# Linear attention and its MLP on one core: k and q of units six to eleven transposed by DMA instead of by TensorE, with a new order

## The chip, the cores and the metric

The kernel runs on one NeuronCore of a Trainium2 chip. TensorE (PE) multiplies matrices into PSUM, VectorE (DVE), ScalarE (ACT) and GpSimd (POOL) work element by element, and SyncE (SP) has no arithmetic of its own: its queue issues transfers, which sixteen DMA engines carry out. Each engine runs its own instructions strictly in the order in which the program gives them and waits at semaphores for the others. The metric is the device time of one execution in microseconds, as a median over runs.

## What is computed

For each of 4 x 8 heads a state of 48 x 48 is carried over 768 steps: it decays by a gate and takes in an outer product, and a query reads it. The 4 x 768 results, 384 numbers each, go through two matrices with a leaky relu between them.

```python
f = 1.0 / (1.0 + np.exp(-f_logit))
for t in range(S):                       # S = 768, D = 48
    state = f[:, :, t, :, None] * state + np.einsum('bhd,bhe->bhde', k[:, :, t], v[:, :, t])
    y[:, :, t] = np.einsum('bhd,bhde->bhe', q[:, :, t], state)
x = y.transpose(0, 2, 1, 3).reshape(B * S, H * D)     # 3072 x 384
h = x @ w_in                                          # 384 x 2048
out = np.maximum(0.01 * h, h) @ w_out                 # 2048 x 384
```

## The kernel before, in words

The sequence is cut into six chunks of 128 steps and the batch into two halves of two batch elements. A chunk of a half is a **unit**; there are twelve, numbered 0 to 11, and `pairs[j]` gives chunk and half of unit `j`. Within a chunk the recurrence becomes matrix products. A unit goes through these steps, each a short function whose name in the order stands in front of it:

- `Lf Lk Lq Lv` (`load`, L99): eight loads per unit, one for each of f, k, q, v and each batch element `a`, all in SyncE's queue. The tiles are ring buffers of six units.
- `gate` (ScalarE): logarithm of the gate. `cs` (TensorE, L141 and L144): its running sum over the chunk, by a product with a triangle of ones. `dec` (ScalarE): the exponentials of it, for k, for q, and for the end of the chunk.
- `k`, `q` (`scale_k` L160, `scale_q` L166): k and q are multiplied by these and rounded to bf16, into tiles `kh` and `qh` of 128 steps x 2 x 8 heads x 64 columns, of which 48 are used and the rest is zero. For units six to eleven GpSimd does both, one instruction for each unit and operand. `v` (`cast_v`, GpSimd) rounds v.
- `tk`, `tq` (`turn`, L187): the scores need k and q with the head's dimension on the partitions. TensorE transposes four blocks of 128 x 128 (two heads each) per batch element into PSUM; `ck`, `cq` (`turn_out`, L190) are VectorE's copies into the tiles `kT` and `qT`.
- `sc` (`score`, L206): products of `kT` and `qT`, for both batch elements of units from four on (`sc_6_2` is unit six, both). `mk` (VectorE, L211): the causal mask. `mx` (`mix`, L239): scores times v, and `qT` times the state from before the chunk. `xt` (VectorE): the result into `xT`.
- `pt` (L250), `sf` (VectorE), `sb` (GpSimd, L260 and L263): the state's update for the next chunk.
- `uu`/`pu` and, from unit four on, `up`/`pr`: the first matrix (L290, L277) and the leaky relu (ScalarE); `dn` (`down`, L300): the second matrix; `ob` (VectorE, L305) and `st` (L313): copy and store.

The weights come in seven pieces through GpSimd's queue (`W`, pieces 0 to 2 of the first matrix, 3 to 6 of the second), from the time when `v` of unit one has landed. `H` (`hold`) is a tiny transfer in SyncE's queue that reads the last bytes of a piece: all that stands behind it in the queue, which is the loads of units two and later, waits until that piece has landed.

Nothing here is scheduled by a tool at build time. `order` is one long text of words, each a call: `tk_6_0` calls `turn(6, 0, "k")`. The order of the words of one engine is that engine's order; between engines the words' order says nothing, the semaphores do. A function `turn_dma` with the words `xk` and `xq` is there and isn't called: it issues one transfer in SyncE's queue that transposes all of a unit's `kh` (or `qh`), 128 x 1024 bf16, straight into `kT` (or `qT`).

Of the kernel before, what the change touches and what calls it, by code (L numbers as in the profile page):

```python
# [15 lines left out]
def kernel(  # L16
# [342 lines left out]
    uu_1_1_3 q_2_0 st_0_0 dn_1_0_1 ob_0_1 sb_1_0 pu_1_1_3 Lf_3_0 k_2_0 tq_2_0 gate_2_1 dn_1_1_0 cq_2_0 sb_0_1 st_0_1
    tk_2_0 pt_2_0 pu_1_1_2 dn_1_1_1 ck_2_0 Lk_3_0 sf_2_0 sb_1_1 sc_2_0 cs_2_1 mk_2_0_1 Lq_3_0 dn_1_1_2 dec_2_1 v_2_1  # L360
    mk_2_0_0 dn_1_0_2 Lv_3_0 mx_2_0 k_2_1 Lf_3_1 gate_3_0 dn_1_0_3 xt_2_0 tk_2_1 q_2_1 Lk_3_1 uu_2_0_0 ck_2_1 tq_2_1
    Lq_3_1 pu_2_0_0 uu_2_0_1 cq_2_1 ob_1_0 cs_3_0 sc_2_1 Lv_3_1 dec_3_0 pt_2_1 mk_2_1_1 dn_1_1_3 st_1_0 mk_2_1_0
    dn_2_0_0 pu_2_0_1 q_3_0 k_3_0 gate_3_1 uu_2_0_2 Lf_4_0 v_3_0 sf_2_1 tq_3_0 tk_3_0 pu_2_0_2 Lk_4_0 dn_2_0_1 ck_3_0
    cq_3_0 cs_3_1 Lq_4_0 mx_2_1 dec_3_1 sc_3_0 xt_2_1 dn_2_0_2 Lv_4_0 k_3_1 q_3_1 uu_2_1_0 Lf_4_1 mk_3_0_0 uu_2_0_3
    v_3_1 pu_2_1_0 ob_1_1 Lk_4_1 pt_3_0 tq_3_1 pu_2_0_3 mk_3_0_1 tk_3_1 uu_2_1_1 st_1_1 ck_3_1 mx_3_0 sf_3_0 pu_2_1_1
    uu_2_1_2 Lq_4_1 cq_3_1 gate_4_0 xt_3_0 dn_2_1_0 Lv_4_1 pu_2_1_2 sc_3_1 cs_4_0 Lf_5_0 mk_3_1_1 uu_3_0_0 dec_4_0
    mk_3_1_0 dn_2_1_1 Lk_5_0 gate_4_1 mx_3_1 k_4_0 q_4_0 Lq_5_0 dn_2_1_2 xt_3_1 v_4_0 pu_3_0_0 cs_4_1 Lv_5_0 uu_3_1_0
    dec_4_1 sb_2_0 dn_2_0_3 Lf_5_1 pu_3_1_0 tk_4_0 q_4_1 ob_2_0 uu_3_1_1 Lk_5_1 ck_4_0 pt_3_1 tq_4_0 pu_3_1_1 sf_3_1
    dn_3_1_0 st_2_0 gate_5_0 uu_3_1_2 cq_4_0 k_4_1 Lq_5_1 pt_4_0 tq_4_1 pu_3_1_2 sf_4_0 cs_5_0 tk_4_1 Lv_5_1 dec_5_0
    uu_3_1_3 ck_4_1 cq_4_1 uu_2_1_3 Lf_6_0 pu_3_1_3 q_5_0 sc_4_2 pu_2_1_3 Lk_6_0 uu_3_0_1 sb_2_1 mk_4_1_1 gate_5_1  # L370
    dn_2_1_3 Lq_6_0 k_5_0 v_4_1 uu_3_0_2 pu_3_0_1 mk_4_0_0 Lv_6_0 dn_3_1_1 mk_4_0_1 v_5_0 pu_3_0_2 cs_5_1 mk_4_1_0
    Lf_6_1 tk_5_0 dec_5_1 uu_3_0_3 ob_2_1 Lk_6_1 mx_4_2 pu_3_0_3 k_5_1 q_5_1 st_2_1 tq_5_0 xt_4_0 dn_3_1_2 v_5_1
    ck_5_0 dn_3_0_0 Lq_6_1 xt_4_1 sb_3_0 tk_5_1 cq_5_0 tq_5_1 Lv_6_1 pt_4_1 ck_5_1 dn_3_0_1 sb_4_0 cq_5_1 Lf_7_0
    up_4_0 sf_4_1 dn_3_0_2 sb_3_1 Lk_7_0 pr_4_0 sc_5_2 Lq_7_0 up_4_1 mk_5_1_0 dn_3_0_3 mk_5_0_0 pr_4_1 Lv_7_0 up_4_2
    mk_5_0_1 gate_6_0 v_6_0 Lf_7_1 dn_3_1_3 mk_5_1_1 pt_5_0 up_4_3 Lk_7_1 pr_4_2 mx_5_2 pr_4_3 Lq_7_1 up_4_4 xt_5_0
    Lv_7_1 cs_6_0 sf_5_0 pr_4_4 up_4_5 ob_3_1 Lf_8_0 sb_5_0 dec_6_0 cs_6_1 up_4_6 xt_5_1 st_3_1 ob_3_0 pt_5_1 pr_4_5
    dn_4_0_0 pr_4_6 up_4_7 st_3_0 dec_6_1 dn_4_0_1 Lk_8_0 up_5_0 pr_4_7 q_6_0 Lq_8_0 dn_4_0_2 gate_7_0 Lv_8_0 up_5_1
# [2 lines left out]
    sf_6_0 pt_6_1 up_5_4 gate_8_0 Lf_9_0 k_7_0 sf_6_1 dn_4_1_0 Lk_9_0 sc_6_2 pr_5_4 up_5_5 q_7_0 Lq_9_0 mk_6_0_0  # L380
    dn_4_1_1 mk_6_0_1 pr_5_5 Lv_9_0 up_5_6 mk_6_1_1 v_7_0 tk_7_0 Lf_9_1 mk_6_1_0 pr_5_6 tq_7_0 dn_5_0_2 ck_7_0 sb_5_1
    Lk_9_1 pt_7_0 tk_7_1 sf_7_0 up_5_7 Lq_9_1 dn_4_1_2 v_8_0 cq_7_0 pr_5_7 ck_7_1 pt_7_1 tq_7_1 Lv_9_1 sf_7_1 cs_8_0
    dn_5_0_3 dec_8_0 cq_7_1 Lf_10_0 mx_6_2 ob_5_0 gate_9_0 st_5_0 dn_5_1_0 xt_6_0 sb_6_0 cs_8_1 xt_6_1 Lk_10_0
    dn_5_1_1 dec_8_1 sb_6_1 up_6_0 Lq_10_0 dn_5_1_2 pr_6_0 Lv_10_0 q_8_0 up_6_1 sc_7_2 Lf_10_1 pr_6_1 up_6_2 mk_7_0_0
    k_8_0 Lk_10_1 dn_5_1_3 mk_7_0_1 pr_6_2 up_6_3 Lq_10_1 mk_7_1_0 tq_8_0 mk_7_1_1 pr_6_3 up_6_4 Lv_10_1 cq_8_0 pt_8_0
    tk_8_0 pr_6_4 ob_5_1 up_6_5 Lf_11_0 sf_8_0 mx_7_2 pr_6_5 st_5_1 ck_8_0 gate_10_0 up_6_6 xt_7_0 Lk_11_0 dn_4_1_3
    xt_7_1 up_6_7 Lq_11_0 pr_6_6 tk_8_1 pr_6_7 tq_8_1 Lv_11_0 ck_8_1 cs_9_0 pt_8_1 ob_4_1 up_7_0 dec_9_0 Lf_11_1
# [2 lines left out]
    pr_7_5 dn_6_0_2 mk_8_1_0 up_7_6 sb_7_0 mk_8_0_0 dn_6_0_3 mk_8_0_1 pr_7_6 k_10_0 tq_9_0 mk_8_1_1 gate_11_0 dn_7_0_2  # L390
    cq_9_0 tq_9_1 mx_8_2 ob_6_0 v_9_0 cq_9_1 st_6_0 dn_6_1_0 xt_8_0 tq_10_0 xt_8_1 sb_7_1 tk_9_0 up_7_7 cq_10_0 ck_9_0
    tq_10_1 sb_8_0 pr_7_7 tk_9_1 cq_10_1 cs_11_0 pt_9_0 up_8_0 dec_11_0 ck_9_1 sf_9_0 dn_7_0_3 sc_9_2 ob_7_0 up_8_1
    mk_9_0_0 st_7_0 dn_7_1_0 mk_9_0_1 dn_6_1_1 mk_9_1_1 dn_7_1_1 mk_9_1_0 cs_11_1 dn_6_1_2 dec_11_1 dn_7_1_2 pr_8_1
# [46 lines left out]
```

## Time and profile before

| | us |
|---|---|
| median of 3 runs (lowest, highest) | 189.87 (189.79, 190.28) |
| the profiled execution | 189.33 |
| its span, first to last instruction | 187.5 |
| TensorE busy / weight loads | 173.9 / 137.9 |
| VectorE, ScalarE, GpSimd busy | 98.3, 99.1, 76.0 |

The page cuts the span into forty slices and shows each engine's busy share in tenths:

```profile
PE   0575899999999999999999999999999999999994
DMA  6999999499997998998998999971110100111122
```

and lists the costliest groups of instructions, with busy time, mean duration, and the idle time ahead of them and who ended it:

```profile
L187 PE MATMUL tp<-ident,kh 128*128 128x128 bf16 x96 | 10.2, 234 | 0.3 <-DVE kh L160 0.2
L187 PE MATMUL tp<-ident,qh 128*128 128x128 bf16 x96 | 10.2, 234 | 2.7 <-DVE qh L166 2.7
L190 DVE COPY kT<-tp 128x512 bf16<-128x512 bf16 x24 | 10.0, 419 | 8.0 <-PE tp L187 7.7
L190 DVE COPY qT<-tp 128x512 bf16<-128x512 bf16 x24 | 10.1, 419 | 7.3 <-PE tp L187 7.0
L160 POOL TENSOR_TENSOR kh<-k_raw,em_t 128x768 bf16<-128x768 f32 x6 | 9.9, 1647 | 7.7 <-issue 7.6
```

A group's busy time is the sum of its instructions' durations; matmuls overlap each other, so for TensorE it is more than the time that they hold the engine. The time of a transfer in the DMA list runs from its issue to its landing.

### The profile page before, as it was taken

The page shows a single profiled execution, that of the slowest core. Times are in us where ns is not written, and L with a number is a line of the kernel's source. Part 1 is how long each engine was busy: PE and PEld are TensorE (multiplying, and loading weights), DVE is VectorE, ACT ScalarE, POOL GpSimd, SP SyncE. Part 2 cuts the span into 40 slices and gives each one's busy share as a digit, 9 for nine tenths or more (in the row PEclk, how much of TensorE's full clock was granted, in tenths as well). Part 3 has the DMA queues.
Part 4 walks back from the last instruction along what each step waited for, and adds up shares of the span by engine and source line. Part 5 has one row for each costly group of instructions (what it writes and reads, how often), then busy time and mean ns, then how long its engine had stood idle before and what let it go on. Part 6 is the DMA issues. An engine that isn't in the chain of part 4 may idle for free.

```text
span 187.5 us, 5631 instructions
## 1 busy us (share of the span) xinstructions
PE 173.9 (93%) x2360; PEld 137.9 (74%) x2360; DVE 98.3 (52%) x212; ACT 99.1 (53%) x201; POOL 76.0 (41%) x138
## 2 busy tenths in 40 slices
PE   0575899999999999999999999999999999999994
...
DMA  6999999499997998998998999971110100111122
GB/s 122 208 207 187 207 213 194 94 188 249 178 237 168 195 223 157 207 209 170 251 233 168 211 192 201 238 147 42 47 45 0 42 5 3 42 42 45 42 84 84
DMA packets 106113, 27.10 MB, mean 145 GB/s; under 512 B 100456, under 2 KB 105192, under 8 KB 106088
## 3 DMA queue, kind: packets, MB, share of 16 engines
...
## 4 chain that ended last, share of the span: by engine, by line
PE 87%; DMA 6%; SPq 3%; issue 2%; POOL 1%; DVE 0%; POOLq 0%
PE po L300 32%; PE pm L277 23%; PE pm L290 13%; PE py L239 5%; PE tp L187 5%; DMA w_in_b<-in_moe_w_in_dram 4%; PE pw L206 3%; SPq L99 3%; DMA v_raw<-in_v_dram 2%; PE cs L141 2%; PE pt L250 2%; PE po L322 1%; PE cs L144 1%; POOL v_b L173 0%; POOL v L174 0%
## 5 line engine op out<-in xcount | busy, mean ns | idle before, releaser
L300 PE MATMUL po<-w_out_b,gT 128*128 128x384 bf16 x368 | 71.6, 326 | 0.0
L283 ACT ACTIVATE gT<-pm 128x512 bf16<-128x512 f32 x64 | 37.6, 598 | 36.0 <-PE pm L277 35.2
L277 PE MATMUL pm<-xT,w_in_b 128*128 128x256 bf16 x384 | 51.4, 273 | 0.0
L300 PEld LDWEIGHTS <-gT 128*128 128x128 bf16 x368 | 34.1, 98 | 16.0 <-issue 0.2
L277 PEld LDWEIGHTS <-w_in_b 128*128 128x128 bf16 x384 | 40.7, 114 | 4.7
L211 DVE TENSOR_TENSOR wm<-pw,ut 128x512 bf16<-128x512 f32 x48 | 30.6, 683 | 19.6 <-PE pw L206 19.4
L305 DVE COPY osb<-po 128x384 f32<-128x384 f32 x23 | 12.6, 551 | 34.4 <-PE po L300 34.3
L295 ACT ACTIVATE gT<-pm 128x512 bf16<-128x512 f32 x32 | 19.1, 595 | 16.5 <-PE pm L290 15.9
L290 PE MATMUL pm<-xT,w_in_b 128*128 128x128 bf16 x384 | 26.8, 225 | 0.5 <-DMA w_in_b<-in_moe_w_in_dram 0.5
L166 POOL TENSOR_TENSOR qh<-q_raw,a_t 128x384 bf16<-128x384 f32 (+1 forms) x12 | 15.7, 1310 | 27.0 <-ACT a_end L155 23.5
L290 PEld LDWEIGHTS <-w_in_b 128*128 128x128 bf16 x384 | 24.3, 116 | 2.3 <-DMA w_in_b<-in_moe_w_in_dram 0.7
L173 POOL CAST v_b<-v_raw 128x384 bf16<-128x384 f32 (+1 forms) x18 | 12.4, 690 | 25.7 <-DMA v_raw<-in_v_dram 25.4
L151 ACT ACTIVATE em_t<-cs 128x384 bf16<-128x384 f32 x24 | 11.7, 490 | 13.1 <-PE cs L144 8.2
L245 DVE CAST xT<-py 128x384 bf16<-128x384 f32 x24 | 12.7, 552 | 7.3 <-PE py L239 6.9
L135 ACT ACTIVATE e_t<-f_raw 128x384 f32<-128x384 f32 (+1 forms) x18 | 11.4, 631 | 9.2 <-DMA f_raw<-in_f_logit_dram 9.2
L263 POOL CAST sb<-sf 64x192 bf16<-64x192 f32 x40 | 14.2, 355 | 4.1 <-PE py L239 1.7
L141 PE MATMUL cs<-lf,ut 128*128 128x384 bf16 x24 | 8.5, 353 | 6.7 <-ACT lf L136 6.5
L190 DVE COPY kT<-tp 128x512 bf16<-128x512 bf16 x24 | 10.0, 419 | 8.0 <-PE tp L187 7.7
L190 DVE COPY qT<-tp 128x512 bf16<-128x512 bf16 x24 | 10.1, 419 | 7.3 <-PE tp L187 7.0
L260 POOL TENSOR_TENSOR sf<-sf,a_end 128x192 f32<-128x192 f32 x20 | 10.4, 518 | 8.0 <-DVE sf L256 7.5
L160 POOL TENSOR_TENSOR kh<-k_raw,em_t 128x768 bf16<-128x768 f32 x6 | 9.9, 1647 | 7.7 <-issue 7.6
L187 PE MATMUL tp<-ident,qh 128*128 128x128 bf16 x96 | 10.2, 234 | 2.7 <-DVE qh L166 2.7
...
## 6 DMA issues: line engine op xcount, KB each, us to landing
f_raw<-in_f_logit_dram SPq DMA_DIRECT2D x24, 192.0 KB, 4.0
k_raw<-in_k_dram SPq DMA_DIRECT2D x24, 192.0 KB, 3.8
q_raw<-in_q_dram SPq DMA_DIRECT2D x24, 192.0 KB, 3.9
v_raw<-in_v_dram SPq DMA_DIRECT2D x24, 192.0 KB, 4.0
out_dram<-osb SPq DMA_DIRECT2D x17, 192.0 KB, 3.2
w_out_b<-in_moe_w_out_dram POOLq DMA_DIRECT2D x4, 384.0 KB, 13.3
...
```

The costliest lines, as they stand in the source:

```text
L166: eng.tensor_mul(qhs[j % NR][:, a, :, 0:D], raw(j, "q")[:, a], st[j]["a"][:, a].rearrange("t a (h d) -> t a h d", d=D))
L187: nc.tensor.transpose(tp[:, p, :], scaled(j, x)[:, a, 2 * p:2 * p + 2, :], ident)
L190: nc.vector.tensor_copy(out=turned(j, x)[:, P2 * a:P2 * a + P2, :], in_=st[j].pop(("tp" + x, a)))
L211: nc.vector.tensor_mul(wm, st[j].pop(("pw", a, i)), ut[:, None, :].to_broadcast([128, P2, 128]))
L245: nc.vector.tensor_copy(out=xT[:, :, a, :], in_=st[j].pop(("py", a))[:, 0:NK, :])
L263: nc.gpsimd.tensor_copy(out=sb[rows, a, :, i * D:i * D + D], in_=sf[rows, a])
L277: nc.tensor.matmul(pm[:, i, :], w_in(kk, ff), st[j]["xT"][:, kk].rearrange("t a s -> t (a s)"), start=(kk == 0), stop=(kk == NK - 1))
L283: nc.scalar.activation(gT[:, 2 * g:2 * g + 2, :], st[j].pop(("pm", g)), AF.Prelu, alpha=0.01)
L290: nc.tensor.matmul(pm[:, i, :], w_in(kk, ff), st[j]["xT"][:, kk, a, :], start=(kk == 0), stop=(kk == NK - 1))
L295: nc.scalar.activation(gT[:, 4 * g:4 * g + 4, 128 * a:128 * a + 128], st[j].pop(("pu", a, g)), AF.Prelu, alpha=0.01)
L300: nc.tensor.matmul(po, st[j]["g"][:, ff, 128 * a:128 * a + 128], w_out_b[:, ff, :], start=(ff == 0), stop=(ff == NF - 1))
L305: nc.vector.tensor_copy(out=osb, in_=st[j].pop(("po", a)))
```

## The change

Units six to eleven use `xk` and `xq` in place of `tk`, `tq`, `ck` and `cq`: twelve DMA transposes in SyncE's queue. `kT` and `qT` have three buffers each and not two. The order of all words is another one, on every engine; in it `H_4` stands in place of `H_5`, and stores of units seven to nine that were cut in two (`st_7_1_2`) are mostly whole. `weights` and `hold` count the pieces of the first matrix by the list's length, which is three as before. The diff, with the order cut to some of its lines:

```diff
@@ -106,12 +106,12 @@
         if (x, j, a) not in seen:
             seen.add((x, j, a))
             nc.gpsimd.tensor_copy(out=gate_w[:, 0:1], in_=raw(j, "fkqv"[x])[0:1, a, H - 1, D - 1:D])
-        if piece < 3:
+        if piece < len(w_in_cols):
             lo, hi = w_in_cols[piece]
             nc.gpsimd.dma_start(out=w_in_b[piece], in_=moe_w_in[:, lo:hi].rearrange("(k p) n -> p k n", p=128))
         else:
             n = NF // 4
-            part = piece - 3
+            part = piece - len(w_in_cols)
             nc.gpsimd.dma_start(
                 out=w_out_b[:, part * n:(part + 1) * n, :],
                 in_=moe_w_out[part * n * 128:(part + 1) * n * 128, :].rearrange("(p a) n -> p a n", a=n))
@@ -120,10 +120,10 @@
 
     def hold(piece):
 
-        if piece < 3:
+        if piece < len(w_in_cols):
             src = w_in_b[piece][0:1, NK - 1, 0:4]
         else:
-            src = w_out_b[0:1, (piece - 2) * (NF // 4) - 1, 0:4]
+            src = w_out_b[0:1, (piece - len(w_in_cols) + 1) * (NF // 4) - 1, 0:4]
         nc.sync.dma_start(out=gate_s[:, 0:4], in_=src)
 
     def half(j, i):
@@ -176,7 +176,7 @@
                               .rearrange("t p (j e) -> t p j e", j=2))
 
     def turned(j, x):
-        return once(j, x + "T", lambda: work.tile([128, 2 * P2, 128], BF16, name=x + "T", tag=x + "T", bufs=2))
+        return once(j, x + "T", lambda: work.tile([128, 2 * P2, 128], BF16, name=x + "T", tag=x + "T", bufs=3))
 
     def scaled(j, x):
         return (khs if x == "k" else qhs)[j % NR]
@@ -346,63 +346,60 @@
 
 
     order = """
...
-    Lk_1_1 k_0_1 tq_0_1 Lq_1_1 mk_0_0_0 tk_0_1 mk_0_0_1 cs_1_0 Lv_1_1 cq_0_1 pt_0_1 dec_1_0 W_0_3_1_0 ck_0_1 mx_0_0
-    W_1_3_1_0 sc_0_1 xt_0_0 gate_1_1 sf_0_1 sb_0_0 q_1_0 cs_1_1 W_2_3_1_0 k_1_0 dec_1_1 tq_1_0 mk_0_1_0 W_3_3_1_0
...
-    uu_1_0_2 uu_1_1_1 pu_1_0_2 H_5 Lf_2_0 dn_0_0_1 pu_1_1_1 Lk_2_0 dn_0_1_1 Lq_2_0 dn_0_0_2 Lv_2_0 uu_1_0_3 Lf_2_1
...
-    k_6_0 dn_4_0_3 Lf_8_1 pr_5_0 tq_6_0 cs_7_0 pr_5_1 cq_6_0 tq_6_1 Lk_8_1 up_5_2 sf_5_1 sb_4_1 dec_7_0 dn_5_0_0
-    ob_4_0 Lq_8_1 up_5_3 pr_5_2 cq_6_1 st_4_0 tk_6_0 pr_5_3 cs_7_1 ck_6_0 tk_6_1 pt_6_0 dec_7_1 dn_5_0_1 Lv_8_1 ck_6_1
...
-    sf_8_1 cs_9_1 up_7_1 pr_7_0 cq_8_1 st_4_1 dn_6_0_0 pr_7_1 up_7_2 Lk_11_1 dec_9_1 dn_6_0_1 Lq_11_1 pr_7_2 cs_10_0
-    q_9_0 up_7_3 dec_10_0 Lv_11_1 cs_10_1 dn_7_0_0 pr_7_3 up_7_4 k_9_0 dec_10_1 dn_7_0_1 pr_7_4 up_7_5 q_10_0 sc_8_2
...
-    pr_9_2 dn_9_0_0 mk_10_1_0 pr_8_5 up_9_3 tk_11_1 pr_9_3 pt_9_1 up_9_4 ck_11_1 sf_9_1 dn_9_0_1 pr_9_4 sb_9_1 up_9_5
-    sc_11_2 pr_9_5 up_9_6 mk_11_0_0 dn_9_0_2 mk_11_1_1 pr_9_6 up_8_6 mk_11_0_1 up_9_7 mk_11_1_0 mx_10_2 pr_9_7 pr_8_6
...
+    mk_0_0_0 gate_1_0 Lk_1_1 q_0_1 mx_0_0 Lq_1_1 k_0_1 cs_1_0 xt_0_0 tq_0_1 Lv_1_1 dec_1_0 tk_0_1 cq_0_1 W_0_3_1_0
+    pt_0_1 ck_0_1 k_1_0 sc_0_1 sb_0_0 gate_1_1 q_1_0 tk_1_0 sf_0_1 W_1_3_1_0 mk_0_1_0 cs_1_1 W_2_3_1_0 dec_1_1
...
+    uu_1_0_1 pu_1_0_0 uu_1_1_0 pu_1_0_1 uu_1_1_1 pu_1_1_0 pu_1_1_1 dn_0_1_0 uu_0_0_2 dn_0_0_0 pu_0_0_2 uu_0_0_3 H_4
...
+    Lf_7_1 up_4_3 pr_4_2 k_6_0 sc_5_2 Lk_7_1 pr_4_3 up_4_4 mk_5_0_0 Lq_7_1 dn_4_0_1 q_6_0 mk_5_1_0 pr_4_4 xk_6 pt_6_0
+    mk_5_0_1 up_4_5 mk_5_1_1 pt_6_1 pr_4_5 up_4_6 xq_6 sf_6_0 mx_5_2 gate_7_0 sf_6_1 Lv_7_1 up_4_7 xt_5_0 sb_5_0
+    dn_4_0_2 Lf_8_0 xt_5_1 pr_4_6 cs_7_0 pr_4_7 up_5_0 dec_7_0 Lk_8_0 cs_7_1 dn_4_0_3 pr_5_0 up_5_1 Lq_8_0 ob_4_0
+    dec_7_1 dn_4_1_0 st_4_0 up_5_2 pr_5_1 q_7_0 sc_6_2 Lv_8_0 pr_5_2 dn_4_1_1 mk_6_0_0 Lf_8_1 up_5_3 sb_5_1 mk_6_1_1
...
+    mk_7_0_1 Lq_9_1 q_8_0 pr_5_7 up_6_5 mk_7_1_1 xk_8 dn_5_0_3 pr_6_5 mx_7_2 ob_5_0 xq_8 dn_6_0_2 gate_9_0 xt_7_0
+    sb_7_0 up_6_6 st_5_0 xt_7_1 pt_8_0 sb_7_1 up_7_0 sf_8_0 Lv_9_1 pr_6_6 pt_8_1 cs_9_0 pr_7_0 sf_8_1 up_7_1 dec_9_0
...
+    st_6_1 up_8_4 mk_9_0_0 dn_8_0_1 Lf_11_1 mk_9_1_0 sb_8_1 pr_8_4 up_8_5 xk_10 mk_9_1_1 pt_9_1 mk_9_0_1 dn_7_0_0
+    pr_8_5 Lk_11_1 sf_9_1 up_8_6 Lq_11_1 mx_9_2 pr_8_6 dn_8_0_2 xt_9_0 sb_9_0 Lv_11_1 up_8_7 xt_9_1 dn_7_0_1 q_10_0
+    pr_8_7 up_9_0 gate_11_0 dn_7_0_2 v_10_0 xq_10 dn_8_0_3 pr_9_0 dn_7_0_3 ob_8_0 sb_9_1 cs_11_0 up_9_1 st_8_0 ob_7_0
+    dec_11_0 dn_7_1_0 st_7_0 v_11_0 pr_9_1 cs_11_1 up_9_2 dec_11_1 dn_9_0_0 pr_9_2 q_11_0 sc_10_2 up_9_3 mk_10_1_0
+    dn_7_1_1 mk_10_1_1 pr_9_3 k_11_0 xq_11 up_9_4 mk_10_0_0 dn_7_1_2 mk_10_0_1 pr_9_4 up_9_5 xk_11 mx_10_2 pr_9_5
+    dn_9_0_1 xt_10_0 up_9_6 xt_10_1 dn_7_1_3 pr_9_6 up_10_0 ob_7_1 sc_11_2 st_7_1 pr_10_0 up_10_1 mk_11_0_1 up_9_7
...
```

More of the change, by code (lines that the diff above doesn't have):

```diff
@@ L354 @@
-    cq_1_1 tk_1_1 uu_0_0_0 mk_1_0_0 ck_1_1 uu_0_1_0 pu_0_0_0 mk_1_0_1 sc_1_1 pu_0_1_0 mk_1_1_0 uu_0_0_1 mx_1_0
-    pu_0_0_1 pt_1_0 xt_1_0 uu_0_1_1 mk_1_1_1 uu_1_0_0 pu_0_1_1 mx_1_1 pu_1_0_0 uu_1_0_1 xt_1_1 pt_1_1 sf_1_0 pu_1_0_1
-    uu_0_0_2 sf_1_1 uu_0_1_2 pu_0_0_2 pu_0_1_2 uu_0_1_3 uu_0_0_3 pu_0_1_3 dn_0_0_0 pu_0_0_3 uu_1_1_0 dn_0_1_0 pu_1_1_0
-    uu_1_0_2 uu_1_1_1 pu_1_0_2 H_5 Lf_2_0 dn_0_0_1 pu_1_1_1 Lk_2_0 dn_0_1_1 Lq_2_0 dn_0_0_2 Lv_2_0 uu_1_0_3 Lf_2_1
-    uu_1_1_2 gate_2_0 Lk_2_1 dn_0_1_2 dn_0_0_3 pu_1_0_3 Lq_2_1 cs_2_0 ob_0_0 dn_0_1_3 dec_2_0 Lv_2_1 dn_1_0_0 v_2_0
@@ L359 @@
[L359 to L377, printed above, removed]
-    k_6_0 dn_4_0_3 Lf_8_1 pr_5_0 tq_6_0 cs_7_0 pr_5_1 cq_6_0 tq_6_1 Lk_8_1 up_5_2 sf_5_1 sb_4_1 dec_7_0 dn_5_0_0
@@ L379 @@
-    ob_4_0 Lq_8_1 up_5_3 pr_5_2 cq_6_1 st_4_0 tk_6_0 pr_5_3 cs_7_1 ck_6_0 tk_6_1 pt_6_0 dec_7_1 dn_5_0_1 Lv_8_1 ck_6_1
[L380 to L387, printed above, removed]
-    sf_8_1 cs_9_1 up_7_1 pr_7_0 cq_8_1 st_4_1 dn_6_0_0 pr_7_1 up_7_2 Lk_11_1 dec_9_1 dn_6_0_1 Lq_11_1 pr_7_2 cs_10_0
@@ L389 @@
-    q_9_0 up_7_3 dec_10_0 Lv_11_1 cs_10_1 dn_7_0_0 pr_7_3 up_7_4 k_9_0 dec_10_1 dn_7_0_1 pr_7_4 up_7_5 q_10_0 sc_8_2
[L390 to L393, printed above, removed]
@@ L394 @@
-    k_11_0 tk_10_0 dn_6_1_3 pr_8_0 ck_10_0 mx_9_2 ob_6_1 q_11_0 st_6_1 up_8_2 xt_9_0 tk_10_1 xt_9_1 pr_8_2 dn_7_1_3
-    v_10_0 tk_11_0 tq_11_0 ck_11_0 up_8_3 ck_10_1 sb_8_1 tq_11_1 cq_11_0 pr_8_3 dn_8_0_0 cq_11_1 up_9_0 v_11_0 up_8_4
-    pr_9_0 sc_10_2 pr_8_4 sb_9_0 up_9_1 mk_10_0_0 dn_8_0_1 mk_10_0_1 pr_9_1 up_9_2 ob_7_1 up_8_5 mk_10_1_1 st_7_1_2
-    pr_9_2 dn_9_0_0 mk_10_1_0 pr_8_5 up_9_3 tk_11_1 pr_9_3 pt_9_1 up_9_4 ck_11_1 sf_9_1 dn_9_0_1 pr_9_4 sb_9_1 up_9_5
-    sc_11_2 pr_9_5 up_9_6 mk_11_0_0 dn_9_0_2 mk_11_1_1 pr_9_6 up_8_6 mk_11_0_1 up_9_7 mk_11_1_0 mx_10_2 pr_9_7 pr_8_6
@@ L399 @@
-    mx_11_2 xt_10_0 up_8_7 xt_10_1 up_10_0 pr_8_7 xt_11_0 dn_9_0_3 xt_11_1 pr_10_0 up_10_1 up_11_0 pr_10_1 dn_8_0_2
-    pr_11_0 up_10_2 up_11_1 pr_10_2 dn_8_0_3 pr_11_1 up_10_3 ob_8_0 up_11_2 ob_9_0 st_8_0_2 pr_10_3 dn_8_1_0 st_9_0_2
-    pr_11_2 up_10_4 dn_8_1_1 pr_10_4 up_10_5 dn_8_1_2 pr_10_5 up_10_6 dn_8_1_3 pr_10_6 up_10_7 ob_8_1 up_11_3 st_8_1_2
-    pr_10_7 dn_9_1_0 pr_11_3 up_11_4 dn_9_1_1 pr_11_4 up_11_5 dn_9_1_2 pr_11_5 up_11_6 dn_9_1_3 up_11_7 ob_9_1
-    dn_10_0_0 st_9_1_2 pr_11_7 dn_11_0_0 pr_11_6 dn_10_0_1 dn_11_0_1 dn_10_0_2 dn_11_0_2 dn_10_0_3 dn_11_0_3 ob_10_0
@@ L404 @@
-    st_10_0_2 dn_10_1_0 ob_11_0 st_11_0 dn_10_1_1 dn_10_1_2 dn_10_1_3 dp_11_1_0 ob_10_1 st_10_1 op_11_1_0 sp_11_1_0
-    dp_11_1_1 op_11_1_1 sp_11_1_1
+    Lf_0_0 Lk_0_0 Lq_0_0 Lv_0_0 Lf_0_1 gate_0_0 Lk_0_1 Lq_0_1 cs_0_0 dec_0_0 Lv_0_1 v_0_0 Lf_1_0 k_0_0 q_0_0 tk_0_0
+    gate_0_1 Lk_1_0 tq_0_0 Lq_1_0 cs_0_1 cq_0_0 ck_0_0 pt_0_0 dec_0_1 Lv_1_0 sc_0_0 sf_0_0 v_0_1 Lf_1_1 mk_0_0_1
+    mk_0_0_0 gate_1_0 Lk_1_1 q_0_1 mx_0_0 Lq_1_1 k_0_1 cs_1_0 xt_0_0 tq_0_1 Lv_1_1 dec_1_0 tk_0_1 cq_0_1 W_0_3_1_0
+    pt_0_1 ck_0_1 k_1_0 sc_0_1 sb_0_0 gate_1_1 q_1_0 tk_1_0 sf_0_1 W_1_3_1_0 mk_0_1_0 cs_1_1 W_2_3_1_0 dec_1_1
@@ new lines @@
+    mk_0_1_1 tq_1_0 W_3_3_1_0 ck_1_0 mx_0_1 W_4_3_1_0 k_1_1 W_5_3_1_0 cq_1_0 tk_1_1 W_6_3_1_0 q_1_1 v_1_0 xt_0_1
+    tq_1_1 ck_1_1 pt_1_0 v_1_1 cq_1_1 sc_1_0 sf_1_0 pt_1_1 uu_0_0_0 mk_1_0_0 mk_1_0_1 sc_1_1 pu_0_0_0 sf_1_1 mx_1_0
+    uu_0_1_0 sb_1_0 mk_1_1_1 uu_0_0_1 xt_1_0 pu_0_1_0 mk_1_1_0 pu_0_0_1 uu_0_1_1 mx_1_1 pu_0_1_1 uu_1_0_0 xt_1_1
+    uu_1_0_1 pu_1_0_0 uu_1_1_0 pu_1_0_1 uu_1_1_1 pu_1_1_0 pu_1_1_1 dn_0_1_0 uu_0_0_2 dn_0_0_0 pu_0_0_2 uu_0_0_3 H_4
+    Lf_2_0 Lk_2_0 uu_1_0_2 pu_0_0_3 Lq_2_0 dn_0_1_1 pu_1_0_2 uu_1_0_3 dn_0_0_1 pu_1_0_3 uu_0_1_2 Lv_2_0 dn_0_0_2
@@ new lines @@
+    pu_0_1_2 uu_0_1_3 Lf_2_1 dn_0_1_2 pu_0_1_3 Lk_2_1 dn_0_0_3 gate_2_0 uu_1_1_2 Lq_2_1 dn_0_1_3 Lv_2_1 cs_2_0 ob_0_1
+    uu_1_1_3 dec_2_0 v_2_0 Lf_3_0 ob_0_0 dn_1_0_0 pu_1_1_2 dn_1_1_0 q_2_0 st_0_0 gate_2_1 dn_1_0_1 k_2_0 st_0_1 tq_2_0
+    tk_2_0 cq_2_0 dn_1_1_1 Lk_3_0 ck_2_0 cs_2_1 sc_2_0 Lq_3_0 dec_2_1 v_2_1 pt_2_0 mk_2_0_0 dn_1_0_2 Lv_3_0 sb_0_1
+    mk_2_0_1 dn_1_1_2 pu_1_1_3 q_2_1 gate_3_0 dn_1_0_3 Lf_3_1 sf_2_0 mx_2_0 Lk_3_1 dn_1_1_3 xt_2_0 tq_2_1 k_2_1 Lq_3_1
+    uu_2_0_0 ob_1_0 cs_3_0 pu_2_0_0 Lv_3_1 uu_2_0_1 cq_2_1 dec_3_0 tk_2_1 v_3_0 uu_2_0_2 st_1_0 ck_2_1 pt_2_1 pu_2_0_1
@@ new lines @@
+    q_3_0 dn_2_0_0 Lf_4_0 sf_2_1 pu_2_0_2 uu_2_0_3 sb_1_1 k_3_0 Lk_4_0 sc_2_1 pu_2_0_3 tq_3_0 mk_2_1_0 Lq_4_0 dn_2_0_1
+    gate_3_1 mk_2_1_1 tk_3_0 dn_2_0_2 Lv_4_0 v_3_1 cq_3_0 cs_3_1 ck_3_0 mx_2_1 Lf_4_1 dec_3_1 ob_1_1 sc_3_0 xt_2_1
+    dn_2_0_3 st_1_1 k_3_1 q_3_1 pt_3_0 uu_2_1_0 mk_3_0_1 Lk_4_1 sb_2_0 tk_3_1 mk_3_0_0 pu_2_1_0 uu_2_1_1 Lq_4_1 sf_3_0
+    dn_2_1_0 pu_2_1_1 Lv_4_1 mx_3_0 v_4_0 gate_4_0 pt_3_1 xt_3_0 tq_3_1 Lf_5_0 uu_2_1_2 gate_4_1 sf_3_1 dn_2_1_1
+    Lk_5_0 ck_3_1 pu_2_1_2 uu_2_1_3 cq_3_1 ob_2_0 Lq_5_0 sc_3_1 pu_2_1_3 cs_4_0 mk_3_1_1 dn_2_1_2 dec_4_0 st_2_0
```

26 lines of the change are left out of this document (23 added, 3 removed).

## The prediction

> **What bounds the kernel now.** I read the table of windows first: it tells in which stretches an engine has no time left.
>
> ```profile
> core 0: us, PE busy (x) PEld busy (x) DVE busy (x) ACT busy (x) POOL busy (x), PEclk, DMA share, GB/s
> 60.00:80.00 20.00, 20.00 (x340) 16.22 (x341) 13.78 (x30) 12.16 (x28) 12.98 (x27) 1.00 0.96 201
> 80.00:100.00 20.00, 20.00 (x254) 16.50 (x253) 11.53 (x26) 15.75 (x32) 11.59 (x15) 1.00 1.01 211
> 100.00:120.00 20.00, 20.00 (x302) 16.28 (x300) 11.91 (x27) 13.37 (x29) 7.69 (x13) 1.00 0.99 200
> 120.00:140.00 20.00, 20.00 (x288) 15.11 (x286) 11.80 (x24) 9.28 (x19) 14.38 (x18) 1.00 0.36 90
> 140.00:160.00 20.00, 20.00 (x296) 17.14 (x294) 9.93 (x20) 9.72 (x17) 5.47 (x13) 1.00 0.04 13
> sum 163.36, PE 163.35 PEld 131.07 DVE 84.19 ACT 89.89 POOL 62.52; mean PE 18.15 PEld 14.56 DVE 9.35 ACT 9.99 POOL 6.95
> ```
>
> The second number of a row is TensorE's busy time: every microsecond from 21.34 to 184.70. The last but one is the DMA engines' share: full until about 123 us, nearly empty after. So there are two full resources, and the change moves work from one to the other. A busy TensorE can hide small gaps, so next the chain of waits in order of time, which shows slots and not durations:
>
> ```profile
> 21.34 2.75 PE pm L290 x24
> ...
> 126.42 0.22 PE tp L187 x4
> 126.64 0.65 PE po L300 x4
> ...
> 129.17 0.45 PE tp L187 x8
> ```
>
> From 21.34 on the chain is TensorE without a break: what leaves TensorE there leaves the end, as long as nothing else comes late. Four transposes hold a slot of 0.22 us (eight: 0.45), although one alone is listed with 234 ns, since they overlap. Last the DMA view of 60 to 100 us and SyncE's timeline:
>
> ```profile
> q1 hardware_dynamic: 37741, 8.15, 98.0%
> ...
> f_raw<-in_f_logit_dram SPq DMA_DIRECT2D x9, 192.0 KB, 4.4
> ```
> ```profile
> 34.38 0.40 SPq L99 DMA_DIRECT2D f_raw<-in_f_logit_dram  x1
> ...
> 121.86 1.14 SPq L99 DMA_DIRECT2D v_raw<-in_v_dram  x1
> ```
>
> SyncE's queue alone fills 98% of the DMA engines. Between these two lines it issues 92 transfers (81 loads, 11 stores) in 88.6 us: 0.96 us each, where an issue that isn't held back takes 0.40.
>
> **What is removed.** Units six to eleven have 6 x 2 x 2 = 24 turns (`tk`, `tq`), each one slot of 0.222 us: 24 x 0.222 = 5.3 us off TensorE, all behind 21.34. With them go 24 copies of 419 ns on VectorE (`ck`, `cq`), 10.1 us; VectorE has 13.78 of 20 us at most in the rows above, so they are worth nothing. The new order also puts a little more work ahead of the first up group. Adding TensorE's slots of all words from `uu_0_0_0` to the end (dn 0.652, up 0.655, uu 0.67, mx 0.90, sc 0.55, pt 0.17, cs 0.26, tk and tq 0.222) gives 158.0 before and 152.4 after: 5.6 us less, 0.3 of it the shift. The old sum took 163.4 us on the chip, so a word's slot is stretched by 1.034.
>
> **What is added.** Twelve transposes in SyncE's queue, each of 128 x 1024 bf16 = 256 KB, from SBUF to SBUF. No row shows one. The lower bound of its DMA time is a load's 0.96 us, if its 1024 rows of 256 B go like a load's 1024 rows of 192 B; by bytes it is 0.96 x 256/192 = 1.28. Less than nothing is excluded: the DMA engines are full. The upper bound is the slowest transfer for its bytes, `w_out_b` with 384 KB in 13.3 us: 8.9 us for 256 KB. I take 1.3, as the loads are the same queue's and the same number of rows; both ends stay for the range.
>
> The Trainium skill, "DMA: Bandwidth & Descriptors", section "Latency and other measured facts", gives a DMA transpose an effective 261 GB/s, by which 256 KB would take an estimated 1.0 us; no run here shows it, and the sum would be the one below.
>
> **Whether they fit.** `xk_6` waits for `k_6` on GpSimd, and behind it in SyncE's queue stand `Lv_7_1` and all loads of units eight to eleven; whoever waits for those is `gate`, `k`, `q`, `v` of these units, then `cs` and `sc` on TensorE, which stand in TensorE's queue ahead of up and down groups that could run. From `xk_6` to `Lv_11_1` the new order has 49.2 us of TensorE slots, times 1.034 = 50.8 us. In that time SyncE must pass 33 loads, 6 stores and 9 transposes. 39 x 0.96 = 37.5 us leave 13.3 us for nine. The loads' last consumers have a little air: from `Lf_11_1` to `gate_11_0` are 5.84 us of TensorE's slots, its landing takes 4.0 (median of that load), 1.9 remain. So:
> - up to (13.3 + 1.9)/9 = 1.69 us a transpose the cost is nothing; the cover is that air, and each 0.1 us beyond costs 0.9 us at the end;
> - the 5.6 us gained are gone at (13.3 + 1.9 + 5.6)/9 = 2.31 us.
>
> At 1.3 us nine take 11.7: they fit. The wait of `xk_6` for `k_6` costs no more, since the span begins at it.
>
> **Landing.** `sc_j` now waits for a DMA. From the last `xk`/`xq` to `sc` the new order has 6.2, 7.0, 7.0, 7.3, 4.4 and 3.6 us of TensorE's slots for units six to eleven. For eleven, `k_11` starts 5.7 us ahead of `sc_11_2` and takes 1.65 (GpSimd's row of 128x768), which leaves 4.0. A load lands in 2.8 us at its fastest, scaled by bytes 3.7. Covered, barely, with DMA engines that are 4% busy there. A landing of 8.9 would stop TensorE for 4.9 us.
>
> **The rest of the new order.** `H_4` lets the loads of unit two start one weight piece earlier (SyncE stood 18.8 us at `H_5`), into engines that were 71% busy: it helps the loads by some 3 us, up to `xk_6`, which then waits for GpSimd; I count nothing. In the head `W_1` stands behind `sb_0_0` (0.51 + 0.74 us on GpSimd): between -1 and +1.3 us, counted as nothing, since the first up group waits for piece zero. For six new waits at places where TensorE had none I add 0.1 us each, 0.6: an estimate, half of the shortest wait in the list of waits (0.2 us) for each.
>
> **Sum.** Span 187.5 - 5.6 + 0.6 = 182.5. The profiled execution took 189.33, 1.83 more than its span, so 184.3; the median of the three runs is 189.87, 0.54 above it, so **184.9 us**.
>
> **Rivals.**
> - *Part of the gain.* A transpose takes 1.7 to 2.3 us or lands a few us too late for units ten and eleven. At 2.0: 9 x 2.0 - 15.2 = 2.8 back, 187.7. For it: the DMA engines were full and the air is 1.9 us. Against it: only nine of twelve stand in the full stretch.
> - *No change.* A landing of 8.9 us on empty engines: 5.6 - 4.9 = 0.7 gained, and with the six small waits 0.1: 189.8.
> - *The DMA queue becomes the bound (slower).* If a transpose takes the queue twice for its bytes, once to read SBUF and once to write it, it costs 2 x 1.28 = 2.6 us. Place: SyncE's queue from `xk_6` to `Lv_11_1`; it decides from 2.31 us on. 9 x 2.6 - 15.2 = 8.2 late at `gate_11`, less 5.6: 192.5. At 4 us it is 9 x 4 - 15.2 - 5.6 = 15.2, 205.1. For it: 98% of these engines are taken already. Against it: a load too is read and written for one price.
> - *The eight blocks go one after another.* A transpose of 128 x 1024 is eight of 128 x 128, and if these aren't spread over the engines it comes near the slowest row, 8.9 us: 9 x 8.9 - 15.2 - 5.6 = 59.3, 249. For it: no row shows how such a transfer is spread. Against it: all loads here use the engines together. The Trainium skill, "VectorE: DVE Perf Modes", section "The three transpose paths", lists 1309 ns for one 128 x 128 DMA transpose; eight in turn would be an estimated 10.5 us, which no run here shows.
>
> **Chances.** Forecast 0.45 (its own range 183.2 to 187), part of the gain 0.13, no change 0.04, queue as the bound 0.23, blocks in turn 0.15. A measurement of this kernel tells about 0.3% (0.57 us) from no change. Faster 0.58, same 0.04, slower 0.38. The range reaches from 183.2 (no new waits, and the head 1 us earlier) to 205 (a transpose of 4 us) and leaves out mostly the last rival.
>
> **What would show it.** Right: 96 matmuls `tp` instead of 192, TensorE still without a gap in every window from its first up group on, `xk`/`xq` issues some 1.3 us apart from their neighbours, landing under 4 us for unit eleven, the last load issued near 135 us. Wrong: ACT's `gate` or TensorE's `pw` and `cs` waiting for DMAs for more than 2 us in all, windows after 85 us with TensorE under 19 of 20, loads that land in 8 us and not 4. The prediction falls if a transpose takes over 2.3 us of the queue.

## The result and the profile after

| | before | after |
|---|---|---|
| median of 4 runs, us | 189.88 | 185.56 |
| ratio, 95% interval | | 0.9771 [0.9745, 0.9797] |
| span of the profiled execution, us | 187.5 | 183.9 |

On two more chips the ratio was 0.9789 [0.9764, 0.9815] and 0.983 [0.9795, 0.9866]. The kernel became 2% faster. The first part of its page counts the instructions:

```profile
PE 169.2 (92%) x2264; PEld 133.1 (72%) x2264; DVE 90.0 (49%) x188; ACT 99.1 (54%) x201; POOL 75.2 (41%) x138
```

2264 matmuls are 96 fewer than the 2360 before, 188 instructions on VectorE 24 fewer than 212. The table of windows, columns as before:

```profile
60.00:80.00 20.00, 20.00 (x365) 16.15 (x364) 15.80 (x34) 14.46 (x33) 12.90 (x27) 1.00 1.01 204
80.00:100.00 20.00, 20.00 (x300) 15.93 (x299) 10.78 (x22) 13.50 (x29) 11.61 (x15) 1.00 1.06 195
100.00:120.00 20.00, 20.00 (x254) 16.49 (x253) 9.01 (x20) 14.50 (x31) 10.80 (x18) 1.00 1.05 199
120.00:140.00 20.00, 20.00 (x267) 15.59 (x266) 9.10 (x18) 11.48 (x20) 10.37 (x16) 1.00 1.01 198
140.00:160.00 20.00, 20.00 (x274) 15.69 (x273) 8.68 (x15) 10.04 (x19) 5.29 (x7) 1.00 0.29 70
```

TensorE is still full in every row. The DMA share has changed most from 120 to 140 us, where it was 0.36 and is now 1.01, and after that from 140 to 160, 0.04 and 0.29. The loads start later by some 14 us (the last one at 136.02, before at 121.86), in time in which the DMA engines had been idle; the first experiment shows that it is the order that puts them there. SyncE's timeline and the DMA view of 84 to 136 us:

```profile
85.75 1.66 SPq L193 DMA_TRANSPOSE kT<-kh  x1
87.52 1.25 SPq L193 DMA_TRANSPOSE qT<-qh  x1
...
136.02 1.66 SPq L99 DMA_DIRECT2D v_raw<-in_v_dram  x1
...
145.57 1.24 SPq L193 DMA_TRANSPOSE qT<-qh  x1
147.17 1.23 SPq L193 DMA_TRANSPOSE kT<-kh  x1
```
```profile
kT<-kh SPq DMA_TRANSPOSE x5, 4.6
qT<-qh SPq DMA_TRANSPOSE x4, 4.5
```

A transpose holds SyncE for 1.23 us even where nothing holds it back (unit eleven, where the engines are nearly idle); a plain load's issue took 0.40. In the full stretch it lands in 4.5 us, a load in 3.6 to 4.1. From the first transpose to the last load are 136.02 - 85.75 = 50.3 us for nine transposes and 38 plain transfers, 39 with the last load itself: at 0.96 us for a plain one, 1.4 to 1.5 us for each transpose, with whatever time SyncE waited among them.

What was not gained stands in the chain of waits of the head:

```profile
14.70 0.89 POOL w_in_b L111
...
15.61 0.65 POOL sf L260
...
16.31 0.34 POOL sb L263
...
16.71 0.35 POOL sb L263
17.06 1.52 POOL w_in_b L111 x2
18.58 2.18 POOL w_out_b L115 x4
...
20.81 0.51 POOL v_b L173
...
21.36 0.48 PE pt L250 x4
21.84 0.54 PE pw L206 x8
...
22.42 0.48 PE pt L250 x4
22.90 1.28 PE pm L290 x12
```

The first up group (`pm`) starts at 22.90 us, before at 21.34. Ahead of it in TensorE's queue stand the state products `pt` of unit one; they need `v` of unit one, and GpSimd gets to it only when it has issued all seven weight pieces. From the first up group to the last matmul were 184.7 - 21.3 = 163.4 us and are 181.1 - 22.9 = 158.2: TensorE's part is 5.2 us shorter, the head 1.6 longer, and the span 3.6 shorter. The head's 1.6 is that of one execution: on the two other chips the first up group of the changed kernel starts at 22.23 and 22.16.

### The profile page after: what moved, and what is told of

It reads as the page before. It is cut to its first block, busy times and chain, and to the rows that moved or that the text cites. A ratio compares the mean times of both kernels' runs of the same rounds, so it can differ in the third digit from the quotient of the medians.

```text
span 183.9 us, 5443 instructions
## 1 busy us (share of the span) xinstructions
PE 169.2 (92%) x2264; PEld 133.1 (72%) x2264; DVE 90.0 (49%) x188; ACT 99.1 (54%) x201; POOL 75.2 (41%) x138
## 3 DMA queue, kind: packets, MB, share of 16 engines
q1 hardware_dynamic: 116408, 26.75, 72.0%
## 4 chain that ended last, share of the span: by engine, by line
PE 87%; POOL 4%; SPq 3%; DMA 2%; issue 2%; DVE 0%; POOLq 0%
PE po L300 33%; PE pm L277 24%; PE pm L290 13%; PE py L239 5%; PE pw L206 4%; SPq L99 3%; DMA v_raw<-in_v_dram 2%; PE pt L250 2%; PE tp L187 2%; PE cs L141 2%; PE po L322 1%; POOL w_in_b L111 1%; POOL w_out_b L115 1%; PE cs L144 1%; POOL v_b L173 1%
## 5 line engine op out<-in xcount | busy, mean ns | idle before, releaser
L290 PE MATMUL pm<-xT,w_in_b 128*128 128x128 bf16 x384 | 27.5, 226 | 0.0
L166 POOL TENSOR_TENSOR qh<-q_raw,a_t 128x384 bf16<-128x384 f32 (+1 forms) x12 | 15.7, 1309 | 14.6 <-ACT a_end L155 8.9
L152 ACT ACTIVATE a_t<-cs 128x384 bf16<-128x384 f32 x24 | 11.9, 494 | 0.0
L136 ACT ACTIVATE lf<-e_t 128x384 bf16<-128x384 f32 (+1 forms) x18 | 11.4, 631 | 0.6
L255 DVE TENSOR_TENSOR sf<-sf,pt 64x192 f32<-64x192 f32 x20 | 6.9, 343 | 9.6 <-PE pt L250 4.3
```

The costliest lines, as they stand in the source:

```text
L166: eng.tensor_mul(qhs[j % NR][:, a, :, 0:D], raw(j, "q")[:, a], st[j]["a"][:, a].rearrange("t a (h d) -> t a h d", d=D))
L290: nc.tensor.matmul(pm[:, i, :], w_in(kk, ff), st[j]["xT"][:, kk, a, :], start=(kk == 0), stop=(kk == NK - 1))
```

## The experiments

Each kernel was timed beside the kernel before on the same chip; its median, the ratio to that and the 95% interval are given. The two more transposes (with `Lf_8_1` moved and without), the idle matmuls and the head's second run had the changed kernel beside them too. The other four were timed beside the kernel before alone, at 188.84 us and not 189.88, so for them the ratio says more than a difference of medians.

**The new order with the turns on TensorE.** Each `xk_j` became `tk_j_0 ck_j_0 tk_j_1 ck_j_1`, and `xq_j` likewise:

```diff
...
-    xk_6
+    tk_6_0 ck_6_0 tk_6_1 ck_6_1
...
```

> The new order as it is, but each xk/xq of units six to eleven is again two turns on TensorE with their two copies on VectorE, at the same place in the order. Theory (TensorE's slots are what was gained): 24 x 0.222 = 5.3 us come back, 185.6 + 5.3 = 190.9 us, a little above the kernel before, since the first up group starts 1.4 us later in the new order. Rival (the new order is the gain, the transposes only ride along): under 187.

Measured: 192.69 us, ratio 1.0207 [1.017, 1.0243], span 190.9. The order is not the gain: without the DMA transposes it is 2% slower than the old one. From its first up group (22.08) to its last matmul (187.88) are 165.8 us, 7.6 more than in the changed kernel. The slots, as the prediction priced them, are 5.3 of these. Another 1.2 are gaps of TensorE, in these windows:

```profile
80.00:100.00 20.00, 19.42 (x257) 15.82 (x255) 11.86 (x26) 11.49 (x27) 10.57 (x13) 1.00 0.74 156
100.00:120.00 20.00, 19.66 (x299) 16.13 (x297) 10.85 (x25) 13.19 (x27) 10.18 (x19) 1.00 0.63 133
120.00:140.00 20.00, 19.71 (x242) 15.67 (x239) 9.49 (x20) 11.49 (x23) 8.37 (x12) 1.00 0.73 156
```

TensorE misses 0.6 + 0.3 + 0.3 = 1.2 us. By its list of waits they are for VectorE: 0.6 us for copies into `kT`, 0.3 for one into `qT`, 0.3 for one into `xT`. The remaining 1.1 us are busy time whose place isn't shown. So more was lost than I expected, and not by the slots alone.

The DMA share falls to 0.63 to 0.74, and yet the last load starts even later than with the transposes:

```profile
138.70 0.84 SPq L99 DMA_DIRECT2D v_raw<-in_v_dram  x1
```

Between 100 and 135 us SyncE's queue stands idle for 4.5 + 4.7 + 1.5 + 5.2 = 16 us, each time ahead of a store that waits for `ob`, with loads behind it. So it is the new order that moves the loads back, and in the changed kernel the transposes take the time that this leaves in the queue.

**The old order with the transposes by DMA.** `tk tq ck cq` of units six to eleven left out, `xk_j` and `xq_j` right behind `k_j_0` and `q_j_0`, three buffers:

```diff
...
-    k_6_0 dn_4_0_3 Lf_8_1 pr_5_0 tq_6_0 cs_7_0 pr_5_1 cq_6_0 tq_6_1 Lk_8_1
+    k_6_0 xk_6 dn_4_0_3 Lf_8_1 pr_5_0 cs_7_0 pr_5_1 Lk_8_1
...
```

> The old order with xk and xq right behind k and q of units six to eleven, turns and copies of these units gone. Theory: TensorE saves 5.3 us, but six transposes stand ahead of the last load in the full queue, 6 x 1.4 = 8.5 us, and the old order leaves the loads of unit eleven about 3.6 us of air, so TensorE waits some 4.9 us: 188.5 to 190.5, with cs of units ten or eleven waiting behind a late gate. Rival (transposes fit anywhere, the order need not know of them): 184.5.

Measured: 192.35 us, ratio 1.0195 [1.0163, 1.0227], span 189.9: slower than before. Its windows from 90 us on:

```profile
90.00:100.00 10.00, 8.56 (x86) 6.34 (x85) 4.45 (x9) 6.26 (x14) 7.04 (x11) 1.00 0.97 197
100.00:105.00 5.00, 5.00 (x98) 3.58 (x96) 2.99 (x7) 1.69 (x5) 3.22 (x8) 1.00 0.98 187
105.00:110.00 5.00, 3.01 (x34) 2.28 (x33) 2.39 (x4) 1.17 (x2) 0.29 (x1) 1.00 0.94 186
110.00:115.00 5.00, 3.12 (x13) 1.88 (x13) 0.46 (x2) 2.91 (x7) 3.24 (x2) 0.54 1.13 245
115.00:120.00 5.00, 5.00 (x86) 3.93 (x84) 1.92 (x5) 3.04 (x5) 0.00 (x0) 0.77 1.08 205
```

With the DMA engines full, TensorE stands 1.4 + 2.0 + 1.9 us, and its granted clock falls to 0.54 and 0.77, which my expectation didn't have. The chain of that stretch runs through SyncE's transposes and the landing of `f`. So the transposes don't fit anywhere: the plan has to need the late loads later, and the new order does. That `cs` of units ten or eleven would be the ones to wait was wrong: the chain has `f` of unit nine, landing at 108.8, and TensorE's longest wait is an up group's for ScalarE's relu, which stands behind that unit's gate.

**Transposes doubled.** A second transpose behind each of units six to nine, into a tile that nobody reads; to make room the scratch tile `e_t` has one buffer:

```diff
+    def turn_again(j, x):
+        out = work.tile([128, 2 * P2, 128], BF16, name="again", tag="again", bufs=2)
+        nc.sync.dma_start_transpose(out=out, in_=scaled(j, x).rearrange("t a h d -> t (a h d)"))
```

> The changed kernel with a second, unused transpose behind each of the eight of units six to nine, into a tile of its own (two buffers; the gate's scratch tile goes from two buffers to one to make room). Theory (in the full stretch a transpose costs the queue 1.4 us; of the 15.2 us that nine may take 12.7 are taken): 8 x 1.4 - 2.5 = 8.7 us late, 194.3, with gates waiting for f. Rival (a transpose costs only its issue, the DMA engines have room for it): no change. Rival (it costs 2.6 us): 204.

Measured: 192.23 us, ratio 1.0184 [1.0147, 1.0221], span 189.6, which is 5.7 above 183.9; TensorE misses 5.8 us in all in the windows from 100 to 160 us. It refutes that a transpose is free and that it costs 2.6 us. SyncE's timeline, first transpose and last load:

```profile
84.82 1.74 SPq L193 DMA_TRANSPOSE kT<-kh  x1
...
145.07 0.90 SPq L99 DMA_DIRECT2D v_raw<-in_v_dram  x1
```

These are 60.3 us apart, 10.0 more for eight: **1.25 us of the queue each**. That is the most direct measurement of the price that the prediction had to bound between 0.96 and 8.9. The single buffer of `e_t` isn't what delays: ScalarE's list of waits has none for that tile, and 13.9 us for `f`, against 5.8 in the changed kernel.

**Two more, and the place of the pinch.** The same for unit six alone:

> The changed kernel with two unused transposes more, behind those of unit six. Theory (eight more delayed the last load by 10 us, 1.25 us each, and the end by 5.7, so 3.3 to 4 us of air are left): 2 x 1.25 = 2.5 us fit, no change within 0.4 us. Rival (no air, each transpose beyond nine goes to the end): 2.5 us more.

Measured: 185.98 us, ratio 0.9867 [0.9827, 0.9907]. The changed kernel beside it:

> The changed kernel itself, for comparison on one chip with the others of this call: 0.977 of the kernel before, with the first up group near 22.7 us.

Measured: 184.77 us, 0.9789 [0.9764, 0.9815]. Neither theory held: 1.2 us of the 2.5 reached the end. ScalarE's timeline, of the changed kernel and of this one, at the gate of unit eight:

```profile
99.16 0.85 ACT L135 ACTIVATE e_t<-f_raw 128x768 f32<-128x768 f32 x1 [0.34 <-DMA f_raw<-in_f_logit_dram]
```
```profile
100.49 0.84 ACT L135 ACTIVATE e_t<-f_raw 128x768 f32<-128x768 f32 x1 [3.14 <-DMA f_raw<-in_f_logit_dram]
```

The brackets show how long ScalarE stood idle ahead of the instruction, and for whom. The first line is from the profile shown in the result, where this gate waits already. In the changed kernel beside this run it starts at 98.17 without a wait, so the two more move it by 2.3 us, nearly all of their 2.5. What TensorE misses is in one window, with the two more:

```profile
100.00:105.00 5.00, 3.82 (x36) 2.93 (x35) 0.60 (x2) 4.45 (x9) 0.61 (x2) 1.00 1.01 188
```

That is the 1.2 us. The air that I had looked for at unit eleven ends at unit eight, right behind the first two transposes. To test this, `Lf_8_1` was moved four places ahead in SyncE's queue, with the two more kept:

```diff
...
-    dn_4_0_2 Lf_8_0 xt_5_1 pr_4_6
+    dn_4_0_2 Lf_8_0 Lf_8_1 xt_5_1 pr_4_6
...
-    mk_6_0_0 Lf_8_1 up_5_3
+    mk_6_0_0 up_5_3
...
```

> The kernel with two transposes more behind those of unit six, and Lf_8_1 moved ahead of Lk_8_0, so that it is issued four places earlier in SyncE's queue. Theory (the two more cost 1.2 us because the f load of unit eight's second half came 3.1 us late at its gate, while later units have air): the gate no longer waits, and the time is back within 0.4 us of the changed kernel, 0.977 to 0.981 of the kernel before. Rival (the queue has no air anywhere beyond nine transposes): the wait only moves to a later unit, and the time stays 1 us above, 0.985 or more.

Measured: 186.7 us, ratio 0.9895 [0.985, 0.994]. The changed kernel beside it:

> The changed kernel once more, for comparison on the same chip: 0.977 to 0.979 of the kernel before.

Measured: 185.13 us, 0.983 [0.9795, 0.9866]. The profiled execution does what the theory says: this gate no longer waits, TensorE is busy 20.00 of 20.00 us in every window from 60 to 160, and the span is 183.9 against 183.4. But two of the four runs have spans of 184.9 and 185.3, the profiled one took 186.69 us, 2.8 more than its span where those of the other three are 1.7 to 1.8, and the median stays 1.6 us above. By the times the rival stands; where those other runs wait isn't known, since only one execution is profiled. This stays open.

**Only the slots.** 16 matmuls into the tiles that `sc` overwrites afterwards, for units six to eleven; they need no transposed data and no copy:

```diff
+            if j >= 6:
+                for i in range(2):
+                    for p in range(P2):
+                        nc.tensor.matmul(st[j]["pw", a, i][:, p, :], ident, ident, start=True, stop=True)
```

> The changed kernel with 16 matmuls of 128x128 by 128 columns ahead of each sc of units six to eleven, into the tiles that sc then overwrites: 96 slots of TensorE as the turns had, without their copies on VectorE and without a new wait. Theory (the slot is the whole gain): 96 x 0.0555 = 5.3 us more than the changed kernel, back to about the kernel before, less what its head is better or worse. Rival (the copies' 10 us on VectorE or the evened order were part of the gain): 3 us or less.

Measured: 191.52 us, ratio 1.0143 [1.0112, 1.0174], 6.7 us more than the changed kernel (184.77; spans 190.0 and 183.3), and not 5.3. TensorE's timeline of one unit:

```profile
94.26 0.61 PE L206 MATMUL pw<-ident 128*128 128x128 bf16 x8
94.80 0.40 PE L210 MATMUL pw<-qT,kT 48*128 48x128 bf16 x8
95.13 0.62 PE L206 MATMUL pw<-ident 128*128 128x128 bf16 x8
95.68 0.40 PE L210 MATMUL pw<-qT,kT 48*128 48x128 bf16 x8
96.01 0.82 PE L304 MATMUL po<-w_out_b,gT 128*128 128x384 bf16 x4
```

From start to start eight idle matmuls hold 0.54 us and the two groups of scores 0.33 each, where sixteen scores in one piece hold 0.55: 96.01 - 94.26 - 0.55 = 1.20 us a unit, 7.2 for six. My 5.3 left out that the scores are split in two here and stand between idle matmuls, four changes of tile form in place of two: eight matmuls in a row hold 0.54 us and not 0.45, the sixteen scores 0.66 and not 0.55. That the changes of form are the reason isn't shown. TensorE stays without a gap, VectorE has none of its copies back, and the whole gain is gone: slots of TensorE are what the change took off the end. That the copies' 10 us left VectorE added nothing that can be seen to the gain over the kernel before. In the new order they wouldn't have been free: with turns and copies the ratio was 1.0207, 0.6% or 1.2 us above this one's, as much as the waits for VectorE found there, though the two intervals overlap a little.

**The head.** `v_1_0` ahead of weight piece four in GpSimd's queue, `pt_1_1` behind the first up group:

```diff
...
-    mk_0_1_1 tq_1_0 W_3_3_1_0 ck_1_0 mx_0_1 W_4_3_1_0 k_1_1 W_5_3_1_0 cq_1_0 tk_1_1 W_6_3_1_0 q_1_1 v_1_0 xt_0_1
-    tq_1_1 ck_1_1 pt_1_0 v_1_1 cq_1_1 sc_1_0 sf_1_0 pt_1_1 uu_0_0_0 mk_1_0_0
+    mk_0_1_1 tq_1_0 W_3_3_1_0 ck_1_0 mx_0_1 v_1_0 W_4_3_1_0 k_1_1 W_5_3_1_0 cq_1_0 tk_1_1 W_6_3_1_0 q_1_1 xt_0_1
+    tq_1_1 ck_1_1 pt_1_0 v_1_1 cq_1_1 sc_1_0 sf_1_0 uu_0_0_0 pt_1_1 mk_1_0_0
...
```

> The changed kernel with v_1_0 ahead of the weight piece four in GpSimd's queue and pt_1_1 behind the first up group in TensorE's. Theory: the missing 1.4 us of the head are TensorE's wait for v of unit one, which stands behind all seven weight issues; the first up group starts at 21.7 and not 22.7, and the end comes 0.6 to 1.1 us earlier: 184.5 to 185.0. Rival (the head is bound by the weights landing, and the first down group then waits for piece three as it lands near 31 us): no change, 185.6.

Measured: 183.56 us, ratio 0.9733 [0.9704, 0.9762]. Beside the changed kernel on another chip:

> The changed kernel with the earlier first up group once more, beside the changed kernel on the same chip. Theory (the head's wait was worth about a microsecond, and the first down group now waits for weight piece three): 0.5 to 1.2 us below the changed kernel. Rival (the first run's gain was that chip's): no difference.

183.61 us, 0.9735 [0.9697, 0.9774], against 184.77 (spans 181.4 and 183.3): 1.2 us faster than the changed kernel by the medians, 1.9 by these spans, 2.7% faster than the one before, the fastest of all. The chain of its head in the second of these runs:

```profile
18.62 0.61 PE tp L187 x4
19.23 0.32 PE pt L250 x4
19.55 0.54 PE pw L206 x5
20.09 1.40 PE pm L290 x12
21.49 0.32 PE pt L250 x4
```

`pt` no longer waits for GpSimd, and the first up group starts at 20.09 us, 2.1 us earlier than in the changed kernel beside it (22.23). The intervals of the two kernels overlap a little; the two runs on two chips agree within 0.1 us. In the first run the chain of the head went on into the landing of weight piece three (29.23 us), for which the first down group waited, so that the next limit is near.

## Why the prediction was right, and where its sizes were off

Forecast 184.9 us, measured 185.56; span 182.5 and 183.9. The mechanism was the one that was put likeliest: TensorE's slots leave the end, and the new order finds room for the transposes in the queue. The two errors of the sum above half a microsecond are sizes, one of them with a wrong wait behind it (the head).

- *TensorE's slots*: 5.6 us predicted, 5.2 measured, and putting idle matmuls back takes the gain away. Right. The sum left out the prediction's own stretch of 1.034, which would have made it 5.8.
- *A transpose's time in the queue*: 1.3 us chosen, by bytes from a load; 1.25 measured by doubling, 1.4 to 1.5 by the plain count. Right, and it decided the case: the break-even was put at 2.3. Both rivals that set the price higher fall with it, the double price of 2.6 and the eight blocks in turn. The Trainium skill, "VectorE: DVE Perf Modes", section "The three transpose paths", by whose 1309 ns a block eight in turn would have been an estimated 10.5 us, differs from the measurement, if it is read so: a whole transpose lands in 3.1 us for unit eleven. The Trainium skill, "DMA: Bandwidth & Descriptors", section "Latency and other measured facts", has its effective 261 GB/s, an estimated 1.0 us, for a middle dimension that isn't contiguous, which the prediction left out; the measured 1.25 us is nearer to it and a little higher.
- *The wait of `xk` for GpSimd*: SyncE stood 14.0 us in all ahead of its transposes, longest 3.1, while the DMA share stayed at 1.01 to 1.06. No cost, as said: the engines live on what is queued.
- *Landing*: 3.1 us for unit eleven, under the 4.0 of cover. Right: TensorE's list of waits has none for a transpose, and neither has that of its weight loads.
- *Six small waits*, 0.6 us: none was found; from 22.90 us on TensorE is busy 158.12 of 158.20. Mis-sized.
- *The head*, "between -1 and +1.3 us, counted as nothing": it cost 1.6 in the profiled execution, 0.8 to 0.9 by the starts on the two other chips. This is the term that made the forecast too low. I had named `W_1` behind `sb_0_0`, and those 1.4 us of GpSimd (15.61 to 17.06) are in the chain. But I counted them as nothing because the first up group waits for piece zero. What it waits for is `pt` of unit one, which the new order puts ahead of it in TensorE's queue, and `pt` waits for a `v` that stands behind `sb_0_0` and all seven weights in GpSimd's. This shift I had booked as 0.3 us gained. Moving the two brought back 1.2 us.
- *The air*, "1.9 remain" at `gate_11`: the sum was right where it was taken and the place wrong. Unit eight's gate had next to none (0.34 and 0.49 us of waiting in two of the three profiles of the changed kernel), and 1.2 of the 2.5 us of two more transposes came through. In the changed kernel itself that cost TensorE nothing.
- *A sign that said nothing*: the prediction named gates that wait for DMAs for over 2 us in all as a sign of being wrong. They wait 5.8 us, and had waited 9.2 before the change: idle time of ScalarE, which wasn't what bounds the kernel.

The predicted sum misses the span by 1.6 (head) + 0.4 (slots) - 0.6 (small waits) = 1.4 us. Outside the span the profiled execution took 1.7 us, not 1.8, and the median lies at that execution and not 0.5 above it, which takes 0.7 off again. That the forecast came within 0.7 us of the measurement is thus in part luck, since errors of 1.6 and 0.4 one way met errors of 0.6 and 0.7 the other way.
